# Second DFT with its even and odd outputs in separate halves of a PSUM tile

## The chip, the cores and the metric

The kernel runs on one core of one Trainium2 chip. The metric is the device time of one execution in microseconds (us). The kernel before was run three times: 322.8, 323.6 and 323.98 us, median 323.6.

## The reference

An attention with sorted key and value blocks gives x of shape (4, 768, 512); an FNet block follows: a Fourier transform over the sequence and over the features, its real part added to x, a layer norm, and a two-layer MLP.

```python
def _moe_ref(x, w_ch1, w_ch2):
    X = np.fft.fft(x, axis=1)
    X = np.fft.fft(X, axis=2)
    mixed = np.real(X).astype(np.float32)
    u = x + mixed
    mu = np.mean(u, axis=-1, keepdims=True)
    var = np.mean((u - mu) ** 2, axis=-1, keepdims=True)
    un = (u - mu) / np.sqrt(var + 1e-06)
    ch = np.maximum(un @ w_ch1, 0.0) @ w_ch2
    return (u + ch).astype(np.float32)
```

The attention before it takes q, k and v of shape (4, 8, 768, 64) and a net of 8 x 8 block weights per head. The weights are made doubly stochastic in five rounds, mix the eight blocks of 96 rows of k and of v, and each block of q then attends to its own mixed block. The heads side by side are x.

## The kernel before

Four batches go through three kinds of work: attention (attn, a_path, a_rows), the Fourier transform and layer norm (fft_ln), and the MLP (mlp). Each is written as a generator; a small planner with estimated durations picks which one goes on, so that the work of batch b's MLP stands between that of batch b+1's attention and transform. The order of instructions within an engine then comes out of a scheduler that works on that stream; each engine runs its own list in order, and semaphores join the engines.

TensorE (PE) does the matmuls. VectorE (DVE) and ScalarE (ACT) share the copies out of PSUM; GpSimd (POOL) computes the small layer-norm factors and issues the loads of q, k, v and the MLP weights; SyncE (SP) issues the constants, the transposes and the stores.

The transform of one batch in fft_ln:

- x of the batch lies in rt (half precision, 768 rows as six tiles of 128, 512 columns). Sums and differences of its parts are made on DVE (pmt, ee, oo, fo), and the first DFT over the sequence runs on PE at line 666 in five pieces of six matmuls, with 193 columns each. ACT copies each result to y and DVE mirrors it to yr, which are then the weights of the second DFT.
- The second DFT runs at lines 738 to 753, once for each of the six row tiles T. A PSUM tile ps of 128 rows and 512 single-precision columns, one bank, takes four matmuls (line 749): each has a weight tile of 128 x 128 out of y or yr, and a table of 256 columns in dtab, which has the columns of the even outputs (c = 0 and 2) and of the odd outputs (c = 1 and 3) apart. Their output is ps[:, c % 2::2], every second column of the bank. A fifth matmul (line 752) adds, over all 512 columns, the mean part of the attention from lt (weights) and rb (512 columns).
- Line 756 on DVE then forms u = x / 1024 + ps, reading rt and PSUM, and lines 759 and 760 make the statistics of the layer norm. After three tiles POOL computes factor and shift (ln_tail), and ACT or DVE normalises u to un (ln_out), which is transposed to ut for the MLP: by PE at line 731 in batch 0, by DMA in the others.

There are six u buffers. A u is kept until line 811 in mlp has added the second MLP product to it and the sum has been stored to out, so that the u of a new batch waits for the store of an old one. The tiles ps come from a ring of five PSUM buffers (pf), which attention and transform share; the MLP and the value mix have a ring of three (pm).

The row rb is made in a_path, once for two batches: PE computes it at lines 528 to 539 in single precision, ACT rounds it (rhi), DVE builds the tile rr with a high and a low part in two blocks (lines 546 to 557), and a_rows copies 32-row pieces of rr to rb by three DMAs per batch. In block 0 the outputs 0 to 256 are computed, even ones in psr[:, 0:129] and odd ones in psr[:, 129:257], and line 552 mirrors them to the outputs 257 to 511. Row 96 of rb is the constant rrow.

Of the kernel before, what the change touches and what calls it, by code (L numbers as in the profile page):

```python
# [13 lines left out]
ALU = mybir.AluOpType  # L14
# [9 lines left out]
DM = 512  # L24
# [3 lines left out]
RSC = 1.0 / XSC  # L28
# [5 lines left out]
def _consts():  # L34
    f16, f32 = np.float16, np.float32
    kd = np.arange(DM)
    dd = np.arange(129)
    ang = 2.0 * np.pi * ((np.outer(dd, kd) % DM).astype(np.float64)) / DM
    ybs = RSC / YSC
    cdm, sdm = np.cos(ang) * ybs, -np.sin(ang) * ybs  # L40
    cdm[0] *= 0.5
    sdm[128] *= 0.5
    dtab = np.stack([cdm[:128, 0::2], cdm[:128, 1::2],
                     sdm[1:, 0::2], sdm[1:, 1::2]], axis=1)
    s_ = np.arange(384)
    k1 = np.concatenate([2 * np.arange(NK), 2 * np.arange(NK) + 1])
    ang = 2.0 * np.pi * ((np.outer(s_, k1) % S).astype(np.float64)) / S
    cs = np.stack([np.cos(ang), np.sin(ang)]).reshape(
        2, 3, 128, 2 * NK).transpose(2, 0, 1, 3)
    kk = np.concatenate([2 * np.arange(129), 2 * np.arange(128) + 1])  # L50
    ang = 2.0 * np.pi * ((np.outer(np.arange(256), kk) % DM).astype(
        np.float64)) / DM
    tab = np.stack([np.cos(ang), np.sin(ang)]).reshape(2, 2, 128, 257)
    tab = tab.transpose(2, 0, 1, 3)
    ii = np.arange(S)
    ang = 2.0 * np.pi * ((np.outer(ii, ii) % S).astype(np.float64)) / S
    csum = np.cos(ang).reshape(S, NB, BLK).sum(2).T
    ssum = -np.sin(ang).reshape(S, NB, BLK).sum(2).T
    ind = np.repeat(np.eye(NB), BLK, axis=1)
    lt = np.zeros((97, S), f16)  # L60
    for o, m in ((0, csum), (32, ssum)):
        hi = m.astype(f16)
        lo = (m - hi.astype(np.float64)).astype(f16)
        lt[o:o + 8] = hi
        lt[o + 8:o + 16] = hi
        lt[o + 16:o + 24] = lo
    lt[64:72] = ind
    lt[72:80] = ind
    rrow = np.cos(np.pi * (kd % 4) / 2)[None, :] * ybs
    pp = np.arange(128)  # L70
    cm = np.zeros((128, 40), f32)
    cm[:, 0:16] = pp[:, None] % 16 == np.arange(16)[None, :]
    cm[:, 16:32] = pp[:, None] // 8 == np.arange(16)[None, :]
    cm[:, 32] = np.where((pp % 32) // 8 == 1, -1.0, 0.0)
    cm[:, 33] = np.where(pp < 64, 1.0, -1.0)

    erow = np.zeros((1, 2 * S), f16)
    for g in range(2):
        for j in range(4):
            erow[0, S * g + 224 * j:S * g + 224 * j + BLK] = 1.0  # L80
    vrow = np.zeros((1, 128, D + 1), f16)
    vrow[0, :, D] = 96.0 / XSC
    vrow = vrow.reshape(1, -1)

    def c(m, t):
        return np.ascontiguousarray(m).astype(t)

    def as32(m):
        return np.ascontiguousarray(m.astype(f16)).view(f32)

    pack = np.concatenate([as32(np.eye(128)), as32(cm[:, 0:16]), cm,
                           np.eye(128, dtype=f32)], axis=1)

    return dict(dtab=c(dtab, f16), cs=c(cs, f16), tab=c(tab, f32),
                lt=np.stack([lt, lt], axis=1),
                rrow=np.tile(c(rrow, f16), (1, 2)),
                erow=np.tile(erow, (1, 4)), vrow=vrow, pack=pack)


# [1 line left out]
def kernel(  # L101
# [10 lines left out]
    nc = tc.nc  # L112
# [11 lines left out]
    def pf(shape, dtype=F32):  # L124
        cnt[0] += 1
        return pfr.tile(shape, dtype, tag="pf", name=f"pf{cnt[0]}")
# [82 lines left out]
    nlo = cm[:, 32:33]  # L209
    sgn = cm[:, 33:34]  # L210

    vcx = const.tile([128, 128, D], F16, name="vcx")
    dtab = vcx[:, 96:112, :].rearrange("p (c w) d -> p c (w d)", c=4)
# [292 lines left out]
    def a_path(t):  # L506
        vb = vbs[t]
        psa = pf([128, 16, NB])
        nc.tensor.matmul(psa.rearrange("p g i -> p (g i)"),
                         vb.rearrange("p a d -> p (a d)"),  # L510
                         bdv32[t].rearrange("p g i -> p (g i)"))
        atd = wt([128, 4, 2, 4, NB], F32, "qt", 3, "atd")
        for h2 in range(2):
            for bb in range(2):
                rows = slice(64 * h2, 64 * h2 + 64)
                src = psa[rows, 8 * bb:8 * bb + 8, :].rearrange(
                    "p (c e) i -> p c e i", e=2)[:, :, h2, :]
                nc.vector.tensor_copy(
                    atd[rows, :, bb, :, :],
                    src[:, :, None, :].broadcast_to([64, 4, 4, NB]))  # L520
        atp = wt([128, 2, 2, 2, 4 * NB], F32, "qt", 3, "atp")
        ad = atd.rearrange("p c b g i -> p c b (g i)")
        nc.vector.tensor_tensor(atp[:, 0], ad[:, 0:2], ad[:, 2:4], op=ALU.add)
        nc.vector.tensor_tensor(atp[:, 1], ad[:, 0:2], ad[:, 2:4],
                                op=ALU.subtract)
        yield op('DVE', 2.0, op('PE', 0.25))
        psx = pf([128, DM])
        for c in range(4):
            nc.tensor.matmul(psx[0:64, 128 * c:128 * c + 128],
                             atd[:, c].rearrange("p b g i -> p (b g i)"), idf)  # L530
        psr = pf([128, 257])
        for o in range(2):
            for par in range(2):
                cs = slice(0, 129) if par == 0 else slice(129, 257)
                for c in range(2):
                    nc.tensor.matmul(
                        psr[64 * o:64 * o + 64, cs],
                        atp[:, par, c].rearrange("p b g -> p (b g)"),
                        tab[:, o, c, cs], start=(c == 0), stop=(c == 1))
        op("PE", 2.8)  # L540
        op("ACT", 1.0)
        op("DVE", 2.2)
        r_ = wt([128, 2, DM], F16, "rr", 1)
        hi = wt([128, DM], F16, "qt", 3, "rhi")
        nc.scalar.copy(hi[:, 0:257], psr)
        nc.vector.scalar_tensor_tensor(
            r_[:, 0, 0:257:2], hi[:, 0:129], nlo, psr[:, 0:129],
            op0=ALU.mult, op1=ALU.add)
        nc.vector.scalar_tensor_tensor(
            r_[:, 0, 1:256:2], hi[:, 129:257], nlo, psr[:, 129:257],  # L550
            op0=ALU.mult, op1=ALU.add)
        nc.vector.tensor_scalar(r_[:, 0, 257:512], r_[:, 0, 255:0:-1], sgn,
                                None, op0=ALU.mult)
        hi2 = wt([128, DM], F16, "qt", 3, "rhi")
        nc.scalar.copy(hi2[0:64], psx[0:64])
        nc.vector.scalar_tensor_tensor(r_[0:64, 1, :], hi2[0:64], nlo[0:64],
                                       psx[0:64], op0=ALU.mult, op1=ALU.add)
        rr[t] = r_

    def a_rows(b):  # L560
# [69 lines left out]
    def fft_ln(b):  # L630
        while b not in attnd:
            yield None
        rt = rts[b]
        lt, rb = lts[b % 2], rbs[b % 2]
# [25 lines left out]
        for ci in range(-1, 4):  # L660
            tab = csa if ci < 2 else sna
            ps = pf([128, 2, NK])
# [12 lines left out]
            if ci >= 0:  # L675
# [7 lines left out]
                                        op0=ALU.mult)  # L683
# [54 lines left out]
        for T in range(6):  # L738
            g, tt = divmod(T, 3)
            if tt == 0:  # L740
                mv = wt([128, 3, 2], F32, "mv", 2)
                ul = []
            while held["u"] >= NU:
                yield None
            held["u"] += 1
            ps = pf([128, DM])
            for c in range(4):
                lh = ys[c][g][:, 128 * tt:128 * tt + 128]
                nc.tensor.matmul(ps[:, c % 2::2], lh, dtab[:, c, :],  # L749
                                 start=(c == 0), stop=False,  # L750
                                 skip_group_check=True)
            nc.tensor.matmul(ps, lt[:, 128 * T:128 * T + 128], rb,  # L752
                             start=False, stop=True, skip_group_check=True)
            t = op("DVE", 1.6, op("PE", 0.66))
            u = wt([128, DM], F32, "u", NU)
            nc.vector.scalar_tensor_tensor(u, rt[:, T, :], RSC, ps,  # L756
                                           op0=ALU.mult, op1=ALU.add)
            st = wt([128, 6], F32, "st", 3)
            nc.vector.bn_stats(st, u)  # L759
            nc.vector.bn_aggr(mv[:, tt, :], st)  # L760
            ul.append(u)
            if tt == 2:
                us[b, g] = ul
                tails.append(ln_tail(g, ul, mv))
            if T == 5:
                fftd[0] += 1
            ndone[0] += 1
            yield clk["PE"] + 0.6
            if T == 4:
                yield from ln_out(0, *tails[0])  # L770
# [228 lines left out]
```

## Time and profile before

| | |
|---|---|
| median of three runs | 323.6 us (322.8 to 323.98) |
| span of the profiled execution, first to last instruction | 321.6 us |
| time of the profiled execution itself | not given by the page; the three runs lie 1.2 to 2.4 us above the span |
| mean granted TensorE clock | 0.968 |
| busy share of PE, DVE, ACT, POOL | 90%, 63%, 38%, 12% |
| second DFT on PE, line 749 | 96 matmuls of 128 x 256 |
| its fifth matmul, line 752 | 24 of 128 x 512 |
| u, line 756 on DVE | 24 of 128 x 512 |

The profile is one execution of the program. Busy time is that of an engine's instructions; for PE the ends of matmuls are modelled, and matmuls overlap in the pipeline, so start-to-start times say more about PE than durations. The chain of waits is followed back from the last instruction and says which engine was waited for at each step. A group row gives line, engine, operation, tiles, shape and count, then busy time and mean duration, then the idle time before those instructions and what ended it. A row of the timeline gives start, duration, engine, line and, in brackets, an idle time before it with its releaser.

### The profile page before, as it was taken

How to read it: one execution, taken by the hardware profiler on the slowest of the kernel's cores; microseconds unless marked ns; L12 is line 12 of the kernel's file. 1: busy time of each engine (PE TensorE's matmuls, PEld its weight loads, DVE VectorE, ACT ScalarE, POOL GpSimd, SP SyncE). 2: the span in 40 equal slices, each digit the busy share in tenths (PEclk: the TensorE clock that was granted, in tenths of full speed). 3: DMA queues.
4: the chain of work that ended last, by engine and by line, in shares of the span. 5: the costliest groups of instructions: out<-in, count | busy, mean ns of one | idle time of the engine just before them, and what ended most of it. 6: DMA issues, size and time to landing. Idle time of an engine off the chain costs nothing.

```text
span 321.6 us, 5938 instructions
## 1 busy us (share of the span) xinstructions
PE 290.4 (90%) x2444; PEld 181.8 (57%) x2444; DVE 203.0 (63%) x454; ACT 122.6 (38%) x254; POOL 40.1 (12%) x73
## 2 busy tenths in 40 slices
PE   0389974699899999999999999999999999999995
PEld 0169853466777776455455656554664564554642
DVE  6795686888795656466495667644943662872831
ACT  2266481568789963012048843210460120110000
POOL 8320051013122010010003000100020010010000
PEclk9986995599999999999999999999999999999999
DMA  8999979971506070102111100021021120121002
GB/s 126 209 290 219 207 122 208 175 103 19 91 3 98 2 100 15 65 34 51 62 48 35 19 33 35 33 51 65 33 51 59 41 51 33 66 48 68 33 2 98
DMA packets 30131, 24.90 MB, mean 77 GB/s; under 512 B 15028, under 2 KB 25780, under 8 KB 30102
## 3 DMA queue, kind: packets, MB, share of 16 engines
q0 software_dynamic: 15552, 13.63, 27.3%
q1 hardware_dynamic: 14552, 10.89, 11.2%
q8 instruction: 19, 0.31, 0.4%
q14 instruction: 8, 0.07, 0.1%
HBM read 29.10 MB, written 6.29 MB: 110 GB/s over the span
## 4 chain that ended last, share of the span: by engine, by line
PE 70%; DMA 9%; ACT 9%; DVE 6%; issue 3%; POOL 2%; POOLq 0%; ACTq 0%
PE pm L802 26%; PE pm L785 24%; DMA q<-in_q_dram 9%; PE pf L749 7%; PE pf L444 4%; ACT ex L408 2%; PE pf L666 2%; PE pf L752 2%; PE pf L400 2%; ACT eb L424 1%; PE pf L375 1%; PE pf L386 1%; ACT vsf L167 1%; ACT un L714 1%; DVE eb L234 1%
## 5 line engine op out<-in xcount | busy, mean ns | idle before, releaser
L785 PE MATMUL pm<-ut,w1sb 128*128 128x384 f16 x512 | 92.5, 327 | 0.0
L802 PE MATMUL pm<-w2sb,hr 128*128 128x512 f16 x384 | 86.8, 379 | 0.0
L785 PEld LDWEIGHTS <-w1sb 128*128 128x128 f16 x512 | 49.8, 100 | 32.9 <-issue 1.2
L802 PEld LDWEIGHTS <-hr 128*128 128x128 f16 x384 | 37.3, 99 | 42.7
L794 ACT ACTIVATE hr<-pm 128x384 f16<-128x384 f32 x47 | 22.9, 493 | 99.1 <-PE pm L785 99.0
L790 DVE TENSOR_SCALAR hr<-pm 128x384 f16<-128x384 f32 x81 | 44.8, 555 | 20.7 <-PE pm L785 17.1
L811 DVE TENSOR_TENSOR u<-pm,u 128x512 f32<-128x512 f32 x24 | 16.5, 687 | 40.9 <-PE pm L802 40.9
L408 ACT ACTIVATE ex<-pf 96x384 f32<-96x384 f32 x64 | 28.2, 489 | 11.8 <-PE pf L400 11.6
L444 PE MATMUL pf<-vsf,eb 97*128 97x96 f16 x384 | 21.3, 211 | 5.5 <-DVE eb L421 4.5
L714 ACT ACTIVATE un<-u,nm,ny 128x512 f16<-128x512 f32 x20 | 15.6, 809 | 25.3 <-POOL nm L702 19.5
L698 POOL TENSOR_SCALAR mv<-mv 128x3 f32<-128x3 f32 x8 | 3.3, 417 | 173.5 <-DVE mv L760 173.5
L444 PEld LDWEIGHTS <-eb 97*128 97x128 f16 x384 | 19.5, 100 | 8.3 <-DVE eb L421 4.6
L424 ACT ACTIVATE eb<-ex,negone 96x384 f16<-96x384 f32 x38 | 23.1, 622 | 0.3
L495 PE MATMUL pm<-bdv,vcx 128*128 128x128 f16 x128 | 21.9, 267 | 1.0 <-DMA vcx<-k_dtab 0.5
L756 DVE SCALAR_TENSOR_TENSOR u<-r,pf 128x512 f32<-128x512 f16 x24 | 16.3, 681 | 9.5 <-DMA out_dram<-u 5.7
L497 PE MATMUL pm<-bdv,vbn 128*128 128x128 f16 x128 | 21.6, 237 | 0.0
L495 PEld LDWEIGHTS <-vcx 128*128 128x128 f16 x128 | 20.1, 173 | 1.3 <-issue 0.9
L497 PEld LDWEIGHTS <-vbn 128*128 128x128 f16 x128 | 17.4, 136 | 0.7 <-issue 0.7
L456 DVE TENSOR_TENSOR r<-pf,rz 128x384 f16<-128x384 f32 x32 | 17.1, 551 | 0.5
L759 DVE BATCH_NORM_STATS2 st<-u 128x6 f32<-128x512 f32 x24 | 16.5, 688 | 0.3
L167 ACT CAST vsf<-pm 96x512 f16<-96x512 f32 x18 | 14.3, 813 | 4.3 <-PE pm L497 4.0
L269 PE MATMUL pm<-vst,pack 128*128 128x512 f16 x12 | 4.2, 501 | 12.2 <-DMA vst<-in_v_dram 12.2
(103 smaller groups left out, 327.5 us busy)
## 6 DMA issues: line engine op xcount, KB each, us to landing
out_dram<-u SPq DMA_DIRECT2D x24, 256.0 KB, 2.0
k<-in_k_dram POOLq DMA_DIRECT2D x8, 384.0 KB, 8.2
q<-in_q_dram POOLq DMA_DIRECT2D x8, 384.0 KB, 9.4
w1sb<-in_moe_w_ch_dram POOLq DMA_DIRECT2D x4, 512.0 KB, 19.6
w2sb<-in_moe_w_ch_dram POOLq DMA_DIRECT2D x4, 512.0 KB, 25.1
vst<-in_v_dram POOLq DMA_DIRECT2D x2, 768.0 KB, 10.7
vcx<-in_v_dram POOLq DMA_DIRECT2D x2, 768.0 KB, 22.7
cs<-k_cs SPq DMA_DIRECT2D x1, 579.0 KB, 13.0
```

Source lines behind the costliest of these rows:

```text
L167: nc.scalar.copy(dst, src)
L408: nc.scalar.activation(ex.rearrange("p j (c r) -> p j c r", r=6), pss[h2][0:96].rearrange("p j (r c) -> p j c r", c=16), AF.Exp, scale=SCALE)
L424: nc.scalar.activation(ed, src, AF.Identity, bias=negone[0:96])
L444: nc.tensor.matmul(po[:, 65 * T:65 * T + 96], e[:, S * g + 256 * tt + 128 * n: S * g + 256 * tt + 128 * n + 128], vsf[:, vi:vi + 96], star ...
L495: nc.tensor.matmul(ps[:, dd, :], vcx[:, :, d], bd, start=True, stop=False)
L497: nc.tensor.matmul(ps[:, dd, :], vbn[t][:, d:d + 1].broadcast_to([128, 128]), bd, start=False, stop=True)
L714: nc.scalar.activation(un, ul[tt], AF.Identity, scale=y[:, tt:tt + 1], bias=nm[:, tt:tt + 1])
L749: nc.tensor.matmul(ps[:, c % 2::2], lh, dtab[:, c, :], start=(c == 0), stop=False, skip_group_check=True)
L785: nc.tensor.matmul(ps, w1sb[:, c, 128 * fc:128 * fc + 128], ut[:, c, :], start=(c == 0), stop=(c == 3))
L790: nc.vector.tensor_scalar(hr[:, fc, :], ps, 0.0, None, op0=ALU.max)
L794: nc.scalar.activation(hr[:, fc, :], ps, AF.Relu)
L802: nc.tensor.matmul(ps, hr[:, fc, 128 * tt:128 * tt + 128], w2sb[:, fc, :], start=(fc == 0), stop=(fc == 15))
```

## The change

The PSUM tile of the second DFT becomes two halves of 256 columns, even outputs in the first, odd ones in the second. The four matmuls of line 749 write one half each, in adjacent columns. Whatever is added to that tile on PE has to have the same order, so the row rrow and the tile rr are built in that order as well: the even half and the odd half of rr's block 0 are each mirrored by an instruction of their own, where one instruction did both before, and block 1 is written through a view that takes the columns apart. Line 756 writes u in the natural order as before, and reads PSUM through a view whose inner step goes from one half to the other.

```diff
@@ -93,7 +93,8 @@
 
     return dict(dtab=c(dtab, f16), cs=c(cs, f16), tab=c(tab, f32),
                 lt=np.stack([lt, lt], axis=1),
-                rrow=np.tile(c(rrow, f16), (1, 2)),
+                rrow=np.tile(np.concatenate([c(rrow, f16)[:, 0::2],
+                                             c(rrow, f16)[:, 1::2]], 1), (1, 2)),
                 erow=np.tile(erow, (1, 4)), vrow=vrow, pack=pack)
 
 
@@ -544,17 +545,22 @@
         hi = wt([128, DM], F16, "qt", 3, "rhi")
         nc.scalar.copy(hi[:, 0:257], psr)
         nc.vector.scalar_tensor_tensor(
-            r_[:, 0, 0:257:2], hi[:, 0:129], nlo, psr[:, 0:129],
+            r_[:, 0, 0:129], hi[:, 0:129], nlo, psr[:, 0:129],
             op0=ALU.mult, op1=ALU.add)
         nc.vector.scalar_tensor_tensor(
-            r_[:, 0, 1:256:2], hi[:, 129:257], nlo, psr[:, 129:257],
+            r_[:, 0, 256:384], hi[:, 129:257], nlo, psr[:, 129:257],
             op0=ALU.mult, op1=ALU.add)
-        nc.vector.tensor_scalar(r_[:, 0, 257:512], r_[:, 0, 255:0:-1], sgn,
+        nc.vector.tensor_scalar(r_[:, 0, 129:256], r_[:, 0, 127:0:-1], sgn,
+                                None, op0=ALU.mult)
+        nc.vector.tensor_scalar(r_[:, 0, 384:512], r_[:, 0, 383:255:-1], sgn,
                                 None, op0=ALU.mult)
         hi2 = wt([128, DM], F16, "qt", 3, "rhi")
         nc.scalar.copy(hi2[0:64], psx[0:64])
-        nc.vector.scalar_tensor_tensor(r_[0:64, 1, :], hi2[0:64], nlo[0:64],
-                                       psx[0:64], op0=ALU.mult, op1=ALU.add)
+        nc.vector.scalar_tensor_tensor(
+            r_[0:64, 1, :].rearrange("p (n m) -> p m n", n=2),
+            hi2[0:64].rearrange("p (m n) -> p m n", n=2), nlo[0:64],
+            psx[0:64].rearrange("p (m n) -> p m n", n=2),
+            op0=ALU.mult, op1=ALU.add)
         rr[t] = r_
 
     def a_rows(b):
@@ -743,18 +749,21 @@
             while held["u"] >= NU:
                 yield None
             held["u"] += 1
-            ps = pf([128, DM])
+            ps = pf([128, 2, DM // 2])
             for c in range(4):
                 lh = ys[c][g][:, 128 * tt:128 * tt + 128]
-                nc.tensor.matmul(ps[:, c % 2::2], lh, dtab[:, c, :],
+                nc.tensor.matmul(ps[:, c % 2, :], lh, dtab[:, c, :],
                                  start=(c == 0), stop=False,
                                  skip_group_check=True)
-            nc.tensor.matmul(ps, lt[:, 128 * T:128 * T + 128], rb,
+            nc.tensor.matmul(ps.rearrange("p n m -> p (n m)"),
+                             lt[:, 128 * T:128 * T + 128], rb,
                              start=False, stop=True, skip_group_check=True)
             t = op("DVE", 1.6, op("PE", 0.66))
             u = wt([128, DM], F32, "u", NU)
-            nc.vector.scalar_tensor_tensor(u, rt[:, T, :], RSC, ps,
-                                           op0=ALU.mult, op1=ALU.add)
+            nc.vector.scalar_tensor_tensor(
+                u.rearrange("p (m n) -> p m n", n=2),
+                rt[:, T, :].rearrange("p (m n) -> p m n", n=2), RSC,
+                ps.rearrange("p n m -> p m n"), op0=ALU.mult, op1=ALU.add)
             st = wt([128, 6], F32, "st", 3)
             nc.vector.bn_stats(st, u)
             nc.vector.bn_aggr(mv[:, tt, :], st)
```

On PE, POOL and SP the list of instructions is the same in both kernels, in the same order. On DVE there are two instructions more, one in each run of a_path, and the scheduler sets the pieces of rr a little differently. DVE in the first a_path, before the change, from the first write of rr (pf are PSUM tiles, eb the attention weights, r the tile rt, rhi the rounded row):

```order
L546 SCALAR_TENSOR_TENSOR rr_565<-rhi_566,pack,pf_556 128x129
L549 SCALAR_TENSOR_TENSOR rr_565<-rhi_566,pack,pf_556 128x128
L455 RECIPROCAL rz_609<-pf_596 128x6
L556 SCALAR_TENSOR_TENSOR rr_565<-rhi_571,pack,pf_551 64x512
L421 TENSOR_SCALAR eb_84<-ex_622 96x4x96
L552 TENSOR_SCALAR rr_565<-rr_565,pack 128x255
L456 TENSOR_TENSOR r_519<-pf_596,rz_609 128x6x64
```

The same place after the change:

```order
L547 SCALAR_TENSOR_TENSOR rr_565<-rhi_566,pack,pf_556 128x129
L550 SCALAR_TENSOR_TENSOR rr_565<-rhi_566,pack,pf_556 128x128
L456 RECIPROCAL rz_610<-pf_597 128x6
L559 SCALAR_TENSOR_TENSOR rr_565<-rhi_572,pack,pf_551 64x256x2
L553 TENSOR_SCALAR rr_565<-rr_565,pack 128x127
L422 TENSOR_SCALAR eb_84<-ex_623 96x4x96
L555 TENSOR_SCALAR rr_565<-rr_565,pack 128x128
L457 TENSOR_TENSOR r_519<-pf_597,rz_610 128x6x64
```

One mirror of 255 columns became two of 127 and 128, and the first of them stands ahead of the write of eb. In the second a_path, near 120 us, DVE before the change has:

```order
L546 SCALAR_TENSOR_TENSOR rr_1964<-rhi_1965,pack,pf_1955 128x129
L549 SCALAR_TENSOR_TENSOR rr_1964<-rhi_1965,pack,pf_1955 128x128
L556 SCALAR_TENSOR_TENSOR rr_1964<-rhi_1970,pack,pf_1950 64x512
L552 TENSOR_SCALAR rr_1964<-rr_1964,pack 128x255
L421 TENSOR_SCALAR eb_84<-ex_2011 96x4x96
```

And after it:

```order
L547 SCALAR_TENSOR_TENSOR rr_1965<-rhi_1966,pack,pf_1956 128x129
L550 SCALAR_TENSOR_TENSOR rr_1965<-rhi_1966,pack,pf_1956 128x128
L553 TENSOR_SCALAR rr_1965<-rr_1965,pack 128x127
L559 SCALAR_TENSOR_TENSOR rr_1965<-rhi_1972,pack,pf_1951 64x256x2
L555 TENSOR_SCALAR rr_1965<-rr_1965,pack 128x128
L422 TENSOR_SCALAR eb_84<-ex_2013 96x4x96
```

Here the first mirror moved ahead of the write of block 1, and all five stand ahead of eb, where four did. On ACT one pair is exchanged, in the attention that runs beside the first a_path: the cast to a ksb tile comes one place earlier, ahead of an exponential (ex) instead of behind it.

## Prediction

> **What bounds the kernel now.** I read the shares of the page first, then the chain of waits, then the busy time by stage.
>
> ```profile
> PE 290.4 (90%) x2444; PEld 181.8 (57%) x2444; DVE 203.0 (63%) x454; ACT 122.6 (38%) x254; POOL 40.1 (12%) x73
> PE 70%; DMA 9%; ACT 9%; DVE 6%; issue 3%; POOL 2%; POOLq 0%; ACTq 0%
> PE pm L802 26%; PE pm L785 24%; DMA q<-in_q_dram 9%; PE pf L749 7%; PE pf L444 4%; ACT ex L408 2%; PE pf L666 2%; PE pf L752 2%; PE pf L400 2%; ACT eb L424 1%; PE pf L375 1%; PE pf L386 1%; ACT vsf L167 1%; ACT un L714 1%; DVE eb L234 1%
> 66.00:85.00 19.00, 17.74 (x224) 12.37 (x218) 14.51 (x40) 14.03 (x31) 3.20 (x6) 1.00 0.61 87
> 85.00:124.00 39.00, 37.56 (x489) 29.59 (x486) 28.57 (x70) 31.96 (x68) 6.24 (x8) 1.00 0.30 45
> 124.00:152.00 28.00, 28.00 (x157) 15.42 (x154) 15.69 (x30) 3.31 (x5) 1.56 (x4) 1.00 0.16 44
> 188.00:215.00 27.00, 27.00 (x228) 16.66 (x226) 18.25 (x40) 7.56 (x15) 1.55 (x4) 1.00 0.13 35
> 240.00:266.00 26.00, 26.00 (x138) 14.02 (x137) 13.81 (x26) 3.31 (x5) 1.55 (x4) 1.00 0.19 51
> ```
>
> The last five rows are stages: start and end, length, then busy time of PE, PEld, DVE, ACT, POOL, the granted clock and DMA. TensorE carries 70% of the chain, and 7% of the span are the matmuls of line 749, the ones that the change alters. The second DFT runs in four bursts of six row tiles (I call one a T: four matmuls of line 749, one of 752). Batch 0's burst lies at 66 to 85 us, where PE, DVE and ACT are all busy for three quarters of the time or more. Those of batches 1 to 3 lie in the other three stages shown, where PE is full at clock 1.00, and DVE has 9 to 12 us to spare in each.
>
> **What a T costs on PE.** The chain lists starts and step times, which are better here than the modelled ends.
>
> ```profile
> 137.22 0.86 PE pf L749 x4
> 183.71 1.04 PE pf L444 x24
> 231.77 0.50 PE pf L666 x6
> 286.77 10.36 PE pm L802 x48
> 297.13 10.40 PE pm L785 x64
> L749 PE MATMUL pf<-vcx,yr 128*128 128x256 f16 x48 | 13.3, 406 | 0.0
> L749 PE MATMUL pf<-vcx,y 128*128 128x256 f16 x48 | 12.8, 408 | 0.0
> L752 PE MATMUL pf<-rb,lt 97*128 97x512 f16 x24 | 10.0, 416 | 0.0
> ```
>
> Line 802 takes 10.36/48 = 0.216 us for 512 columns, 0.422 ns a column. Line 785 takes 10.40/64 = 0.1625 us for 384, 0.423 ns. Line 666 takes 0.50/6 = 0.083 us for 193, 0.432 ns. All three write contiguous columns. Line 749 takes 0.86/4 = 0.215 us for 256 columns: 0.84 ns, just double, and also shows the same duration as line 752, which has twice the columns. Its moving operand, dtab, is contiguous and its type is the same; what sets it apart is that it writes every second PSUM column. After the change it writes 256 adjacent ones, so I price it at 256 x 0.423 = **0.108 us**. The weight load in front of each matmul can't hold it above that: line 444 runs a load and a matmul every 1.04/24 = 0.043 us.
>
> The saving is 0.215 - 0.108 = 0.107 us a matmul, 0.43 us a T, and 24 x 0.43 = 10.3 us of PE time in all: 7.7 us in the 18 Ts of batches 1 to 3, 2.6 us in the 6 of batch 0. By line 666's rate it would be 0.05 us a batch less. Line 752 keeps its 512 contiguous columns: nothing.
>
> **What DVE pays.** The sum u (line 756) now reads PSUM with a pair from two places 1,024 bytes apart. No instruction of before does just this, so I bound it by strided and contiguous reads of PSUM.
>
> ```profile
> L756 DVE SCALAR_TENSOR_TENSOR u<-r,pf 128x512 f32<-128x512 f16 x24 | 16.3, 681 | 9.5 <-DMA out_dram<-u 5.7 <-PE pf L752 3.8
> L811 DVE TENSOR_TENSOR u<-pm,u 128x512 f32<-128x512 f32 x24 | 16.5, 687 | 40.9 <-PE pm L802 40.9
> L790 DVE TENSOR_SCALAR hr<-pm 128x384 f16<-128x384 f32 x81 | 44.8, 555 | 20.7 <-PE pm L785 17.1
> L169 DVE CAST ksb<-pf 128x384 f16<-128x384 f32 x9 | 5.0, 551 | 1.7 <-PE pf L375 1.6
> L169 DVE CAST vsf<-pm 96x512 f16<-96x512 f32 x14 | 11.1, 800 | 4.4 <-PE pm L497 4.4
> L677 ACT ACTIVATE y<-pf 128x386 f16<-128x386 f32 x16 | 7.7, 507 | 0.4 <-PE pf L666 0.4
> L794 ACT ACTIVATE hr<-pm 128x384 f16<-128x384 f32 x47 | 22.9, 493 | 99.1 <-PE pm L785 99.0
> ```
>
> The cast to ksb reads with an inner step of 128 words and takes 551 ns; line 790 reads as many elements in order and takes 555. ACT's line 677 reads exactly such interleaved halves, in steps of 193 words, at 507 ns for 386 columns against 493 for 384 in order. The dearest row is the cast to vsf, 800 ns against 687 for 512 elements, but it also scatters its output in runs of 4. So the lower end is -4 ns, the upper end +113 ns; I take 0, since the two rows nearest in form show none.
>
> Would that price matter? In batches 1 to 3 the tightest place is the loop of line 811, the write of out, and the next u, which needs that u buffer.
>
> ```profile
> 128.41 0.69 DVE L811 TENSOR_TENSOR u<-pm,u 128x512 f32<-128x512 f32 x1 [0.73 <-PE pm L802]
> 131.31 0.69 DVE L756 SCALAR_TENSOR_TENSOR u<-r,pf 128x512 f32<-128x512 f16 x1 [2.22 <-DMA out_dram<-u]
> 132.72 0.69 DVE L811 TENSOR_TENSOR u<-pm,u 128x512 f32<-128x512 f32 x1
> 137.26 0.69 DVE L811 TENSOR_TENSOR u<-pm,u 128x512 f32<-128x512 f32 x1 [0.23 <-PE pm L802]
> ```
>
> From the first to the second row of line 811 DVE and DMA need 132.72 - 128.41 = 4.31 us. PE's round (a T and 16 matmuls of line 802) takes 1.08 + 3.46 = 4.54 us now and will take 4.11, so DVE falls 0.2 us behind in each of two rounds, 0.4 us by the third line 811. PE feels that only through the three pm buffers: the third one is wanted again by the third group of line 785, a T and two groups later (0.65 + 2 x 0.65 = 1.95 us), while line 811 ends about 0.9 us after its matmul. That leaves 1.05 us against 0.4, or against 0.4 + 2 x 0.11 at the upper price. So the cover holds and all **7.7 us** count.
>
> **Batch 0.** Here DVE holds PE's gain back.
>
> ```profile
> 67.38 0.69 DVE L756 SCALAR_TENSOR_TENSOR u<-r,pf 128x512 f32<-128x512 f16 x1 [0.52 <-PE pf L752]
> 70.44 0.20 DVE L455 RECIPROCAL rz<-pf 128x6 f32<-128x6 f32 x1 [0.18 <-PE pf L444]
> 77.40 1.52 ACT L714 ACTIVATE un<-u,nm,ny 128x512 f16<-128x512 f32 x2
> 79.60 0.58 ACT L167 COPY ut<-pf 128x512 f16<-128x512 f16 x1 [0.68 <-PE pf L731]
> 81.42 0.68 PE L444 MATMUL pf<-vsf,eb 97*128 97x96 f16 x12 [0.86 <-ACT ut L167]
> 82.78 1.03 PE L749 MATMUL pf<-vcx,yr 128*128 128x256 f16 x4
> 84.06 0.69 DVE L756 SCALAR_TENSOR_TENSOR u<-r,pf 128x512 f32<-128x512 f16 x1 [0.88 <-PE pf L752]
> ```
>
> From 67.4 to the statistics of tile 2, DVE waits only twice for PE, 0.52 and 0.18 us. The first wait shrinks by 0.43, the second goes: 0.61 us. ACT's un at 77.40 starts that much earlier, at 76.8; it needs 1.52 us, so ends at 78.3. In the row of 79.60 ACT waits 0.68 us for the transposes of line 731, which sat behind PE's backlog of five Ts; PE now arrives before un, so this wait goes as well and ut starts at 78.3, 1.3 us earlier. Line 444 at 81.42 waits for ut, so PE gains 1.3 us there, and the last T adds 0.43: **1.7 us** by the u at 84.06. What follows to 124 us hangs on that u, its LN tail and ACT's queue, and I carry the 1.7 through. Its bounds are 0 and the full 2.6 us.
>
> **The rr tile.** DVE gets two more instructions in all, because the mirror (line 552) is cut in two, and the order shifts a little.
>
> ```profile
> L552 DVE TENSOR_SCALAR rr<-rr,pack 128x255 f16<-128x255 f16 x2 | 0.6, 278 | 0.0
> 50.87 0.36 DVE L281 COPY qr<-q 128x768 f16<-128x768 f16 x1 [3.96 <-DMA q<-in_q_dram]
> ```
>
> The extra piece costs between nothing and 0.28 us each time. The first time it runs near 42 us, with ACT's exchanged pair near it, and DVE's wait of 3.96 us for q hides both; if q were early, it would cost at most 0.28. The second time is near 120 us, amid waits of DVE on ACT; I take 0, at most 0.2. The other rr writes become contiguous or strided on the same few rows; the DMAs to rb are the same three per batch. At 0, with the piece's bounds kept.
>
> **The sum.** 7.7 + 1.7 = 9.4 us off the span of 321.6: 312.2 us. The page gives no time for the profiled execution beyond its span. The three runs are 322.8 to 323.98, median 323.6, so 2.0 us lie outside the span or in scatter, and the change doesn't touch them: 323.6 - 9.4 = **314.2 us**.
>
> **Rivals.**
>
> *All of it (0.10).* If batch 0 gives its whole 2.6 us, because ACT and DVE rather than line 444's wait also start earlier after 85 us: 323.6 - 10.3 = 313.3. Against it: DVE is busy 14.5 of 19 us there.
>
> *DVE reads the pairs at half rate (0.12).* From 384 to 512 columns DVE's rows rise by 687 - 555 = 132 ns for 128 elements, 1.03 ns each; a second access for each adds 512 x 1.03 = 0.53 us per u. In batch 0 five u's stand ahead of the statistics of tile 2 and one more at 84.06, so 6 x 0.53 = 3.2 us are lost there. In the loop above, line 811 would be 0.4 + 2 x 0.53 = 1.46 us late against 1.05 of cover, 0.4 us in each of three batches. 314.2 + 3.2 + 1.2 = 318.6. The Trainium skill, "Advanced Engine Details and Errata", section "PSUM Cachelines", says that PSUM has lines of two fp32 values and that consecutive elements should be adjacent in pairs; held against the new read it speaks against the change, since every element then changes line, and would give this rival's time. The trace's strided reads (551 against 555 ns) don't show such a price on DVE, so it gets no more than this.
>
> *The read is dearer still, and DVE sets the pace (0.03): slower.* With an added price d per u, the loss is 6d in batch 0 and 3 x (0.4 + 2d - 1.05) later. At d = 0.95 us it equals 9.4, so a u of over 1.63 us decides. At d = 1.6 it is 9.6 + 7.7 = 17.3 us: 331.5. Nothing in the rows comes near: the dearest adds 0.113.
>
> *PE is not faster (0.04).* If the 0.215 us comes from something other than the step of the output, for instance that these matmuls accumulate, the change does nothing: about 323.6. Against it: line 752 accumulates into the same tile at 512 columns in the same time.
>
> **The numbers.** My forecast, 314.2 us, holds 0.71: with the unknowns it runs from 313.3 to 315.9 (batch 0 gives all or nothing), or 314.9 with the upper price of the read in batch 0 (6 x 0.113 = 0.7). With the runs' scatter of about 0.6 us on either side this is 312.7 to 316.5; to reach 8 in 10 with part of the half-rate rival I set 312.7 to 317.0. Over 0.5% (1.6 us, about what a measurement of this kernel can tell from no change) faster: 0.71 + 0.10 + 0.12 = 0.93; within it: 0.04; slower: 0.03.
>
> **What would show it.** The group of line 749's matmuls should step at 0.108 us, four of them in 0.43, and its chain share should fall from 7% to about 3.5%. The u group should stay at 680 ns; 790 is the upper price, 1,200 the half-rate rival. The stages of batches 1 to 3 should each be about 2.6 us shorter with PE full, and the wait of u for out_dram should grow by some tenths, since u waits for the same write from an earlier time. At the end of batch 0's burst the time should be 1.7 us ahead, with new short waits of PE on ACT's un. The forecast is wrong if PE shows waits on DVE at line 785 after a burst, or if the gain of batch 0 is gone by 124 us.

## The result and the profile after

| | before | after |
|---|---|---|
| median, us | 323.52 (322.8 to 323.98) | 314.29 (314.12 to 314.84) |
| span of the profiled execution, us | 321.6 | 312.7 |
| ratio after / before | | 0.9717, 95% interval 0.9702 to 0.9733 |

The median before is that of four runs here, the three of above and one more. The change saves 9.2 us; 314.2 was forecast. The changed kernel's shares and its chain of waits by engine and by line, then the rows of the second DFT (line 755 was 749, line 758 was 752), of u (line 763, was 756) and of the write of rr's block 1 (line 559, was 556):

```profile
PE 283.5 (91%) x2444; PEld 180.0 (58%) x2444; DVE 204.6 (65%) x456; ACT 123.2 (39%) x254; POOL 40.6 (13%) x73
PE 74%; ACT 9%; DVE 8%; DMA 4%; POOL 2%; issue 1%; POOLq 0%; ACTq 0%; DVEq 0%
PE pm L811 26%; PE pm L794 23%; PE pf L445 5%; PE pf L755 3%; DMA vst<-in_v_dram 3%; PE pm L270 3%; ACT ex L409 2%; PE pm L496 2%; PE pf L401 2%; PE pm L498 2%; PE pf L672 2%; PE pf L387 2%; PE pf L758 2%; ACT eb L425 2%; PE pf L376 2%
...
L763 DVE SCALAR_TENSOR_TENSOR u<-r,pf 128x512 f32<-128x512 f16 x24 | 16.3, 680 | 8.1 <-DMA out_dram<-u 5.7 <-PE pf L758 2.1
...
L758 PE MATMUL pf<-rb,lt 97*128 97x512 f16 x24 | 9.2, 381 | 0.0
...
L755 PE MATMUL pf<-vcx,yr 128*128 128x256 f16 x48 | 8.2, 273 | 0.1
L755 PE MATMUL pf<-vcx,y 128*128 128x256 f16 x48 | 7.7, 272 | 0.0
...
L559 DVE SCALAR_TENSOR_TENSOR rr<-rhi,pack,pf 64x512 f16<-64x512 f16 x2 | 4.9, 2464 | 0.0
```

The share of the four matmuls in the chain fell from 7% to 3%. The duration of line 755 fell from 407 to 273 ns, that of u stayed where it was (681 and 680). One row moved that I had not priced: the write of rr's block 1 rose from 717 to 2,464 ns. Its row before:

```profile
L556 DVE SCALAR_TENSOR_TENSOR rr<-rhi,pack,pf 64x512 f16<-64x512 f16 x2 | 1.4, 717 | 0.0
```

The chain by time after the change shows the step of the four matmuls, start and length in us:

```profile
127.52 3.46 PE pm L811 x16
130.98 0.44 PE pf L755 x4
131.42 0.22 PE pf L758
131.63 3.46 PE pm L811 x16
135.09 0.44 PE pf L755 x4
135.53 0.22 PE pf L758
...
148.12 1.94 PE pm L811 x9
```

Four matmuls take 0.44 us in place of 0.86, so 0.11 us each, and PE goes on without a gap. Each burst of batches 1 to 3 lies between two groups of the MLP's second product, which start in the chain of before at 124.44, 151.94, 214.92 and 265.72, and after at 123.15, 148.12, 208.57 and 256.82. The stages between them took 27.50, 62.98 and 50.80 us before, 24.97, 60.45 and 48.25 after: 2.5 us less for each burst.

### The profile page after: what moved, and what is told of

Its sections match the earlier page's. It is cut to its first block, busy times and chain, and to the rows that moved or that the text cites. A ratio compares the mean times of both kernels' runs of the same rounds, so it can differ in the third digit from the quotient of the medians.

```text
span 312.7 us, 5938 instructions
## 1 busy us (share of the span) xinstructions
PE 283.5 (91%) x2444; PEld 180.0 (58%) x2444; DVE 204.6 (65%) x456; ACT 123.2 (39%) x254; POOL 40.6 (13%) x73
## 4 chain that ended last, share of the span: by engine, by line
PE 74%; ACT 9%; DVE 8%; DMA 4%; POOL 2%; issue 1%; POOLq 0%; ACTq 0%; DVEq 0%
PE pm L811 26%; PE pm L794 23%; PE pf L445 5%; PE pf L755 3%; DMA vst<-in_v_dram 3%; PE pm L270 3%; ACT ex L409 2%; PE pm L496 2%; PE pf L401 2%; PE pm L498 2%; PE pf L672 2%; PE pf L387 2%; PE pf L758 2%; ACT eb L425 2%; PE pf L376 2%
## 5 line engine op out<-in xcount | busy, mean ns | idle before, releaser
L794 PEld LDWEIGHTS <-w1sb 128*128 128x128 f16 x512 | 48.7, 98 | 31.3 <-issue 1.3
L445 PE MATMUL pf<-vsf,eb 97*128 97x96 f16 x384 | 22.1, 216 | 0.9 <-ACT ut L168 0.9
L445 PEld LDWEIGHTS <-eb 97*128 97x128 f16 x384 | 20.2, 103 | 3.3 <-issue 1.2
L270 PE MATMUL pm<-vst,pack 128*128 128x512 f16 x12 | 5.5, 630 | 12.7 <-DMA vst<-in_v_dram 12.7
```

The costliest lines, as they stand in the source:

```text
L445: nc.tensor.matmul(po[:, 65 * T:65 * T + 96], e[:, S * g + 256 * tt + 128 * n: S * g + 256 * tt + 128 * n + 128], vsf[:, vi:vi + 96], star ...
L794: nc.tensor.matmul(ps, w1sb[:, c, 128 * fc:128 * fc + 128], ut[:, c, :], start=(c == 0), stop=(c == 3))
```

## The experiments

Two theories of the whole were set against each other. In mine the 9.2 us are PE's halved step, 7.7 us from batches 1 to 3 and about 2 from batch 0, and the DVE side is free or nearly so. The rival left room for a loss: the traces show batch 0's burst starting 0.8 us later after the change (66.92 against 66.11), and the dear write of rr could be why, so that a better write would gain more.

**The PE part alone.** The kernel before, with only the output of line 749 changed; the columns of the transform are then added to x in another order.

```diff
-                nc.tensor.matmul(ps[:, c % 2::2], lh, dtab[:, c, :],
+                nc.tensor.matmul(ps[:, 256 * (c % 2):256 * (c % 2) + 256],
+                                 lh, dtab[:, c, :],
```

> The kernel before with only the PE part of the change: line 749 writes even and odd outputs to halves, u reads PSUM in order (so the columns of the transform are added in another order), rr and rrow as before. If the whole gain is PE's and the interleaved read costs nothing: 313.5 to 314.3, line 749 stepping at 0.108 us. If DVE's read costs 0.1 us each: 0.7 us less than the changed kernel. If PE's 0.215 us does not come from the step of the output: 323.5.

Measured: 313.83 us (313.17 to 314.16), ratio 0.9692 (0.9672 to 0.9712). The whole gain is there, with PE's part alone. It is 0.5 us under the changed kernel, but the two intervals overlap; this kernel has neither the interleaved read nor the new writes of rr, and both are tried below.

**The read alone.** The kernel before, with u reading the two halves of ps interleaved, PE as before; the columns are taken in another order.

```diff
+                u.rearrange("p (m n) -> p m n", n=2),
+                rt[:, T, :].rearrange("p (m n) -> p m n", n=2), RSC,
+                ps.rearrange("p (n m) -> p m n", n=2),
```

> The kernel before with only the read of the change: PE writes every second column as before, u reads its two halves interleaved (so the columns are taken in another order). If the read is free, u stays at 681 ns and the time at 323.5. At half rate u takes 1,210 ns; then some 4 us more, 328.

Measured: 323.5 us, ratio 0.9997 (0.9988 to 1.0007). The group row of u in that run:

```profile
L756 DVE SCALAR_TENSOR_TENSOR u<-r,pf 128x512 f32<-128x512 f16 x24 | 16.3, 680 | 9.6 <-DMA out_dram<-u 5.7 <-PE pf L752 3.7
```

680 ns where it was 681: the interleaved read costs DVE nothing.

**Pairs.** What sets the step: any gap in the output, or single columns? The kernel before, with line 749 writing two adjacent columns and leaving out two; the columns come out in another order.

```diff
+                po = ps.rearrange("p (m n w) -> p n m w", n=2, w=2)[:, c % 2]
+                nc.tensor.matmul(po, lh,
+                                 dtab[:, c, :].rearrange("p (m w) -> p m w", w=2),
```

> The kernel before, but line 749 writes runs of two adjacent columns and leaves out two (even outputs in columns 0, 1, 4, 5 and so on, odd ones in 2, 3, 6, 7), u reads in order; the columns come out in another order. If PSUM takes a pair of adjacent columns at a time, two single columns cost as much as two pairs, and a step of 0.108 us follows: 313.5 to 314.3. If any gap halves the rate, the step stays 0.215 us and the time 323.5. If each break between runs costs a fixed time, something between: 0.16 us, 318.5.

Measured: 314.17 us, ratio 0.9704 (0.9688 to 0.9720). Its matmuls in the chain and as groups:

```profile
129.97 0.44 PE pf L750 x4
134.08 0.44 PE pf L750 x4
...
L750 PE MATMUL pf<-vcx,yr 128*128 128x256 f16 x48 | 8.2, 273 | 0.1
L750 PE MATMUL pf<-vcx,y 128*128 128x256 f16 x48 | 7.7, 273 | 0.0
```

Pairs with gaps of two are as fast as 256 adjacent columns; single columns with a gap of one cost double. So a gap as such is not what costs. The reading that PE writes two adjacent columns, 8 bytes, at a time fits all three; other gaps and run lengths were not tried.

**Batch 0 apart from the others.** The changed kernel, with the old output and the old read in some bursts; their mean part is then misplaced, since rb keeps the new order. For batch 0 the edit is as below, for batches 1 to 3 it has b == 0 instead, and u reads to match.

```diff
+                po = (ps[:, c % 2, :] if b > 0 else
+                      ps.rearrange("p n m -> p (n m)")[:, c % 2::2])
+                nc.tensor.matmul(po, lh, dtab[:, c, :],
```

> The changed kernel, but batch 0's burst writes every second PSUM column and reads them in order as before (its rb stays in the new order, so batch 0's mean part is misplaced). The difference to the changed kernel is what batch 0 gives: 1.7 us by the prediction, so 316.0; 2.1 us by the two traces (burst 1.29 us earlier at its end after starting 0.8 us later), so 316.4; 2.6 us if DVE holds nothing back, 316.9; 314.3 if batch 0 gives nothing.

> The changed kernel, but the bursts of batches 1 to 3 write every second PSUM column and read them in order as before (their rb stays in the new order, so their mean part is misplaced). If the three bursts give all of 18 x 0.43 = 7.7 us, this is 322.0 to 322.2 us where the changed kernel is 314.3 to 314.5. If DVE holds some of it back, less: 321 or under.

Measured: with batch 0 as before 316.60 us, ratio 0.9777 (0.9763 to 0.9792); the changed kernel beside it had 314.59, so batch 0 gives 2.0 us. With batches 1 to 3 as before 321.88 us (320.78 to 322.99, a wider scatter than the others), ratio 0.9955 (0.9935 to 0.9975); the changed kernel beside it had 314.31, so they give 7.6. Together 9.6, against 9.2 to 9.4 for the whole in three measurements.

**The write of rr.** First in the changed kernel: the same values, written half by half, so that the output lies in adjacent columns and the inputs are read at step 2. Beside it the changed kernel itself.

```diff
-            r_[0:64, 1, :].rearrange("p (n m) -> p m n", n=2),
-            hi2[0:64].rearrange("p (m n) -> p m n", n=2), nlo[0:64],
-            psx[0:64].rearrange("p (m n) -> p m n", n=2),
+            r_[0:64, 1, :].rearrange("p (n m) -> p n m", n=2),
+            hi2[0:64].rearrange("p (m n) -> p n m", n=2), nlo[0:64],
+            psx[0:64].rearrange("p (m n) -> p n m", n=2),
```

> The changed kernel, but the write of rr's block 1 goes through it half by half (output in adjacent columns, inputs at step 2) instead of alternating between two places 512 bytes apart; same result, same order of instructions. The write took 2,464 ns after the change against 717 before. Theory A, the dearer write delayed the start of batch 0's burst by the 0.8 us that the profile of after shows (66.92 against 66.11): 313.5 us, the write near 720 ns. Theory B, the wait for q hides it and the 0.8 us comes from the slower first 40 us of that one execution: 314.3, no change.

> The changed kernel unaltered, run beside the next three so that each has it on the same chip. Expected 314.3 us, 9.2 less than the kernel before; both theories say the same.

The row of the write in the first of these, with the new order:

```profile
L559 DVE SCALAR_TENSOR_TENSOR rr<-rhi,pack,pf 64x512 f16<-64x512 f16 x2 | 1.4, 715 | 0.0
```

The write is back at 715 ns. The times are 314.04 us (313.15 to 314.73) with it and 314.59 (313.75 to 315.31) without: ratios to before 0.9695 (0.9678 to 0.9712) and 0.9714 (0.9697 to 0.9731), whose intervals overlap. The reverse was run beside them, the kernel before with the alternating write (the low part of rb then has its columns in another order):

> The kernel before, with only the alternating write of rr's block 1 from the change, so that the low part of rb has its columns in another order. Theory A: up to 0.8 us more than before, 324.3. Theory B: 323.5. On both the write takes some 2,460 ns.

Measured: 323.86 us, ratio 1.0002 (0.9992 to 1.0012). The write there, and DVE's next wait for q, which is a row of the timeline (start, duration, then the idle time before it):

```profile
L556 DVE SCALAR_TENSOR_TENSOR rr<-rhi,pack,pf 64x512 f16<-64x512 f16 x2 | 4.9, 2456 | 0.0
...
50.79 0.36 DVE L281 COPY qr<-q 128x768 f16<-128x768 f16 x1 [2.57 <-DMA q<-in_q_dram]
```

The write takes 2,456 ns there and the time doesn't move: it eats 1.4 us of the 3.96 that DVE waited for q, and 2.57 are left. A second pair followed:

> The changed kernel once more, beside the next run, to settle a difference of 0.5 us that was within the scatter: 314.3 to 314.6.

> The same kernel as rr_runs, with the write of rr half by half. If the alternating write costs time in the changed kernel, 0.5 us less than the changed kernel beside it again; if the wait for q hides it, as the kernel before with the alternating write shows (1.0002), no difference.

Measured: 314.31 us for the changed kernel, 314.35 with the better write; ratios 0.9712 and 0.9716. The 0.55 us of the first pair did not come again, so the medians show no gain of the better write; a few tenths of a us would be lost in their scatter.

**Where the 0.8 us came from.** In part from the write, in the profiled execution of after. The first part of before, PE and then DVE, as timeline rows:

```profile
15.97 0.53 PE L375 MATMUL pf<-bdk,k 128*64 128x128 f16 x12 [0.78 <-DVE bdk L353]
16.77 1.46 PE L269 MATMUL pm<-vst,pack 128*128 128x512 f16 x6
...
40.98 0.36 DVE L546 SCALAR_TENSOR_TENSOR rr<-rhi,pack,pf 128x129 f16<-128x129 f16 x1
```

The same in after. The rows of PE and the row of line 559 are from its chain, which gives start and length; the others are from the timeline:

```profile
16.47 0.85 PE pf L376 x12
18.08 2.56 PE pm L270 x6
...
43.78 0.34 DVE L547 SCALAR_TENSOR_TENSOR rr<-rhi,pack,pf 128x129 f16<-128x129 f16 x1
44.48 2.35 DVE rr L559
51.00 0.34 DVE L282 COPY qr<-q 128x768 f16<-128x768 f16 x1
59.75 1.15 PE pf L672 x6
```

In after, PE ran the early matmuls at a slower pace for longer: the twelve of line 376 took 0.85 us and the six of line 270 took 2.56, where before they took 0.53 and no more than 1.46. So the first write of rr starts 2.80 us later, at 43.78. That leaves 1.16 us of the 3.96 that DVE waited for q before, and the write of block 1, 1.75 us longer, doesn't fit under it. Line 282 no longer waits for q, line 559 stands on the chain, and the first DFT starts 0.64 us later (59.75 against 59.11). The remaining 0.2 us to the start of the burst were not traced. This execution, 314.84 us, is the slowest of the four; a third profile of the changed kernel has line 559 on its chain as well.

In the second profile of the changed kernel DVE comes to rr earlier, at 42.33, and the wait for q covers the same write, with 0.90 us to spare:

```profile
42.33 0.34 DVE L547 SCALAR_TENSOR_TENSOR rr<-rhi,pack,pf 128x129 f16<-128x129 f16 x1
50.53 0.36 DVE L282 COPY qr<-q 128x768 f16<-128x768 f16 x1 [0.90 <-DMA q<-in_q_dram]
58.77 1.15 PE pf L672 x6
```

There the burst starts at 65.90, ahead of before's 66.11, and the time is the fastest of its four, 313.75 us. With the better write it starts at 66.53 and 66.61 in its two profiles, though 1.92 and 2.22 us of the wait are left there, so single executions differ by some tenths without the write too. The write is a cost that shows only where its cover is short.

Why PE's early pace lasted longer in after was not tried. It looks like half clock, but the profile lists a granted clock of 1.00 from 16 to 22 us in both. The half-clock stretch that follows (0.56 and 0.50 in 22 to 29 us before, 0.50 in 26 to 32 us after) adds nothing to the delay: line 375's next group starts 2.97 us later in after, ahead of that stretch (20.51 against 23.48), and the first write of rr 2.80 us later, behind it. The Trainium skill, "TensorE: Matmul & The Clock Gate", section "What's actually happening", says that the window by which the clock is set runs free and doesn't start with the kernel. A low stretch that moves between executions agrees with that; what shifted it was not tried.

## Why the prediction was right

- **The step of line 749: right.** 0.108 us was forecast from contiguous rows, and 0.44/4 = 0.11 was measured. The reason given, that writing every second column costs double, holds in a sharper form: pairs are free, single columns are not. The weight load (98 ns each) didn't surface.
- **Batches 1 to 3: right.** 7.7 us forecast, 7.6 measured, and 2.5 us in each of the three stages, where about 2.6 was named.
- **The loop of u, the store of out, and line 811: right in its end.** The lines of after, line 820 being the old 811:

```profile
127.02 0.69 DVE L820 TENSOR_TENSOR u<-pm,u 128x512 f32<-128x512 f32 x1 [0.62 <-PE pm L811]
129.90 0.69 DVE L763 SCALAR_TENSOR_TENSOR u<-r,pf 128x512 f32<-128x512 f16 x1 [2.19 <-DMA out_dram<-u]
131.23 0.68 DVE L820 TENSOR_TENSOR u<-pm,u 128x512 f32<-128x512 f32 x1
135.44 0.67 DVE L820 TENSOR_TENSOR u<-pm,u 128x512 f32<-128x512 f32 x1
```

  DVE's rounds are 4.21 us (127.02 to 131.23 to 135.44) against PE's 4.11, where 4.31 was forecast, so DVE falls behind by 0.1 us a round and not by 0.2. Line 820 no longer waits for PE in the third round, as it did for 0.23 us, and PE waits nowhere: the cover by the pm buffers held. The wait of u for out was to grow by some tenths and did not, 5.7 us in both: that sign was wrong. A round is now set by DVE and the store, whose wait is about as long as it was (2.19 against 2.22 us).
- **What DVE pays for the read: right at 0**, by the read alone.
- **Batch 0: right in its mechanism, its size off by 0.3 to 0.4 us.** From the first T to the last 16.67 us passed before (66.11 to 82.78) and 14.99 after (66.92 to 81.91), 1.7 less, where 1.3 was forecast; with the last T's 0.42 that is 2.1, and 2.0 by the experiment. The rows of after:

```profile
66.92 0.61 PE L755 MATMUL pf<-vcx,y 128*128 128x256 f16 x4
77.21 1.52 ACT L720 ACTIVATE un<-u,nm,ny 128x512 f16<-128x512 f32 x2 [0.83 <-POOL nm L708]
78.73 0.59 ACT L168 COPY ut<-pf 128x512 f16<-128x512 f16 x1
80.55 0.68 PE L445 MATMUL pf<-vsf,eb 97*128 97x96 f16 x12 [0.86 <-ACT ut L168]
81.91 0.60 PE L755 MATMUL pf<-vcx,yr 128*128 128x256 f16 x4
```

  ACT now waits for POOL ahead of un, its wait for the transposes ahead of ut (0.68 us) is gone, and line 445 still waits for ut: the path that was named. But un stands 10.29 us behind the first T, before 11.29: DVE and POOL came out 1.0 us earlier, not 0.61. The mis-sized term is DVE's waits for PE: only the two that the timeline names were counted, and they gave 0.70 of the 1.0: 0.40 at the first u (1.27 us behind the first T, then 0.87) and 0.30 at the second RECIPROCAL (70.10 to the statistics at 70.55 before, 70.41 to 70.56 after). Two more show only in the starts. The second and the fifth u started before at 69.40 and 74.07, each 0.04 us after line 752's matmul had ended (68.94 + 0.42 and 73.61 + 0.42). The second u gained 0.09 us on the first (2.02 us behind it, then 1.93), the fifth 0.16 us on the fourth (1.34, then 1.18).
- **The rr tile: wrong in its price, right in its effect on the medians only.** I took the writes of rr for nearly unchanged and bounded only the extra mirror (at most 0.28 us); the alternating write took 1.75 us more, twice. What I named as cover, the wait for q, hid the first in the kernel before with that write (1.0002) and in the second profile of the changed kernel. In the first profile the cover was short, and some 0.6 us were lost; I had bounded that case at 0.28. The second write, near 118 us, is hidden: from the last u of batch 0's burst to the first long group of the MLP's second product is 40.38 us in both profiles (84.06 to 124.44, and 82.77 to 123.15).
- **The sum** of 9.4 stands between the 9.2 to 9.4 of the whole and the 9.6 of the parts. That it was right to 0.1 us is in part luck: batch 0 was priced 0.3 us too low, batches 1 to 3 0.1 us too high, and the write of rr, put at nothing, cost some 0.6 us in one profiled execution.

## What to carry over

The step of a matmul's output can double its time: compare its start-to-start time per column with that of a contiguous matmul of the same kernel, and move a reordering from PE's write, where it cost 0.1 us a matmul, to a read on the engine with room, where it was free. If a gap is needed on PE, leave it between pairs of adjacent single-precision columns. When an order changes, price each writer that has to follow it by its own form, look for what covers it, and see in more than one profile how long that cover is.

## What was not expected of the hardware

- PE wrote 256 single-precision columns in 0.215 us as every second column, in 0.11 us as pairs with gaps of two, and in 0.11 us adjacent. The Trainium skill, "Advanced Engine Details and Errata", section "PSUM Cachelines", says that any access that isn't contiguous slows matmuls, and that every two consecutive elements should be adjacent. The pairs show that the second is enough for PE here; the first is too broad. Held against DVE's interleaved read it would have spoken against the change, and that read cost nothing (680 ns against 681).
- On DVE a half-precision output that alternates between two places 512 bytes apart took 2,464 ns for 512 elements, against 715 for the same values in two runs with the inputs at step 2: (2,464 - 715) / 512 = 3.4 ns more an element for the write, none for the reads. The Trainium skill, "Vector Engine (DVE) Microarchitecture Reference", section "Measured stream behaviour on trn2", paragraph "The SBUF access granule: adjacent pairs", has destinations that hop at each 4-byte word at up to 2.51 ns a column in all. The half-precision one here took 2,464 / 512 = 4.8 ns, so it is dearer.
